# Attention and two expert layers on one core: high parts of the last layer's operands one step ahead of their low parts, and second products in another order

## The chip, the core and the metric

The kernel runs on one core of a Trainium2 chip. Its engines are TensorE (PE, which also loads weights, shown as PEld), VectorE (DVE), ScalarE (ACT), GpSimd (POOL) and SyncE (SP), which here only issues DMAs. Each engine works through its own list of instructions in the order written. The metric is device time of one execution in microseconds (us): the kernel before takes 1069.21 us, the median of 3 runs (1068.4 to 1069.44).

## The reference

```python
def _moe2_ref(x, w_in, w_out, s, b):
    h = x @ w_in                  # 2304 x 512 by 512 x 2048
    r = np.maximum(h, 0.0)
    g = s * (r * r) + b
    return (g @ w_out).astype(np.float32)

def reference(**kwargs):
    attn_out = _attn_ref(**attn_kwargs)          # two softmax attentions
    x = attn_out.transpose(0, 2, 1, 3).reshape(B * S, H * D)
    x = _moe_ref(x=x, **moe_kwargs)              # four experts, weighted sum
    return _moe2_ref(x=x, **moe2_kwargs)         # the last layer
```

Everything is float32. The change lies in the last layer alone, `_moe2_ref`.

## The kernel before

**Stages.** Attention comes first, then the four experts, then the last layer. Every float32 product is made of three reduced-precision matmuls: an operand is split into a high part (ACT copies it, rounded) and a low part (DVE or POOL subtracts the high part from the source), and the products low x high, high x high and high x low are added up in PSUM.

**The last layer.** The 2048 hidden columns are four groups `g` of 512, and the 2304 tokens three passes `tp` of 768. Each pair (group, pass) is a block scheme with seven products in the place of eight, `k` from 0 to 6, named 11, 12, s2, s1, s3, s4 and 22 in the order of work, and each has two column blocks `j`. That makes 4 x 3 x 7 x 2 = 168 steps. One step issues the six matmuls of one first product (`m3`, line 1053, 384 columns each). For a group after the first, nine matmuls of the *second* products of the pass before follow in the same step (`m4_next`, line 1191, 256 columns each). A pass is 14 steps.

**Second products.** They too are seven products in a block scheme, in the order of the tuple `LAST` (line 697). Product `k` takes the gated activation `gg[g, tp, k]` and the weight `wov[g, k]`, and has three row blocks `i` of 128 tokens with six matmuls each: 18 matmuls in two steps. The function `behind` (line 1582) writes this list, row blocks in the order 0, 1, 2. The products form two chains in PSUM. Chain a is 11, s2, s3, 22 and adds up in bank `on_0`; chain b is 12, s1, s4 in bank `on_2`. Row blocks 0 and 2 lie in the chain's bank; row block 1 of both chains lies in one common bank, `on_1`, each chain in its own half. A finished row block is added to the result by DVE (line 1206): once for row block 1 (128x256) and once for row blocks 0 and 2 together (128x512). The next matmul into a bank waits for the write-outs of that bank, whichever half they read.

**What else DVE and ACT do in a pass.** The first products go to SBUF as `z` (DVE lines 1119, ACT lines 1110 to 1128). After step 10 of a pass come its squares (ACT, line 1133) and the scaling by `s` and `b` (ACT, line 1135), then four sums of blocks (DVE, line 1147, tiles `qs` and `z`), then the high part (ACT) and the low part (DVE, line 1159) of each `gg`. These stand in the weave at fixed steps: `q_sum` at steps 16, 16, 18 and 19 counted from the pass's start, `q_part` for product k at step 13 + 2k (high) and 14 + 2k (low), both for k = 0 at 13 and 14 and for k = 1 the same.

**The first-weight operands.** Seven operands `wop[g, k]` per group are made in the last pass of the group before: POOL makes sums of weight blocks (`wi_sums`, lines 774 to 781), and `wop_parts` (line 783) makes high and low parts in two halves `j`, ACT at line 789 (128x256) and DVE at line 790. For operand k both stand at step u0 + 2k + 1, where u0 is the first step of that pass. An operand is used 14 steps after its step u0 + 2k.

**What sets the order.** The order on each engine is the order in which the Python code issues instructions: a dictionary from step to functions (`at`, `run`), then the step's first product, then its nine second products. Nothing reorders it later.

Of the kernel before, what the change touches and what calls it, by code (L numbers as in the profile page):

```python
# [9 lines left out]
F32R = mybir.dt.float32r  # L10
U32 = mybir.dt.uint32
AF = mybir.ActivationFunctionType
ALU = mybir.AluOpType
# [6 lines left out]
def attention_experts_mlp_kernel(  # L20
# [25 lines left out]
    nc = tc.nc  # L46
# [5 lines left out]
    P = 128  # L52
# [12 lines left out]
    NS = T3 // P  # L65
# [5 lines left out]
    keep = ctx.enter_context(tc.tile_pool(name="keep", bufs=1))  # L71
# [10 lines left out]
    def f32(ap):  # L82
        return ap.bitcast(F32)
# [607 lines left out]
    NQ = FG // 2  # L691
    HK = KB // 2

    OPS = ("11", "12", "s2", "s3", "s1", "s4", "22")
    NK = len(OPS)
    ORDER = ("11", "12", "s2", "s1", "s3", "s4", "22")
    LAST = ("12", "11", "s2", "s1", "s3", "s4", "22")
    wi_dram = [dram.tile([P, 2, DM], F32, name=f"wi_dram{q}") for q in range(DFF // P // 2)]
    wo_dram = [dram.tile([P, DM], F32, name=f"wo_dram{fb}") for fb in range(DFF // P)]

# [49 lines left out]
    tw, wop = {}, {}  # L750
# [29 lines left out]
                nc.gpsimd.tensor_tensor(out=t2, in0=t["s4"], in1=t["s1"], op=ALU.subtract)  # L780
                nc.gpsimd.tensor_tensor(out=t4, in0=t4, in1=t2, op=ALU.subtract)

    def wop_parts(g, k):
        n = g * NK + k
        tag = "w1" if n % 8 < 4 else "w1p"
        t = wop[g, k] = keep.tile([P, NQ, 2, HK * P], F32R, tag=tag, bufs=4, name=f"wop{g}{k}")
        for j in range(NQ):
            src = tw[g * NQ + j][(ORDER if g else OPS)[k]]
            nc.scalar.activation(t[:, j, 0], src, AF.Copy)
            nc.vector.tensor_tensor(out=t[:, j, 1], in0=src, in1=f32(t[:, j, 0]), op=ALU.subtract)  # L790

    def wo_tile(fb):
        t = wodd.tile([P, 2, DM], F32R, tag="w1p", bufs=FG, name=f"wo{fb}")
# [33 lines left out]
    def wov_parts(g, k):  # L827
        pool, tag = (gb, "wo") if ((g - 1) * NK + k) % 8 < 4 else (wodd, "w1p")
        t = wov[g, k] = pool.tile([P, 2, 2, HK * P], F32R, tag=tag, bufs=FG, name=f"wov{g}{k}")
        hi, lo, src = t[:, 0], t[:, 1], tv[g][LAST[k]]  # L830
        nc.scalar.activation(hi, src, AF.Copy)
# [318 lines left out]
    def q_part(g, tp, k, n):  # L1150
        src = quad[g, tp][LAST[k]]
        if n == 0:
            gg[g, tp, k] = gb.tile(
                [P, 2, 2, T3], F32R, tag="gg", bufs=6, name=f"gg{g}{tp}{k}"
            )
            nc.scalar.activation(gg[g, tp, k][:, 0], src, AF.Copy)  # L1156
        else:
            t = gg[g, tp, k]
            nc.vector.tensor_tensor(out=t[:, 1], in0=src, in1=f32(t[:, 0]), op=ALU.subtract)  # L1159
# [21 lines left out]
    def m4_next(g, tp, k, i, n):  # L1181
        op = LAST[k]
        b = int(op in ("12", "s1", "s4"))
# [29 lines left out]
    with tc.manual_schedule():  # L1213
# [8 lines left out]
        for gi in range(G):  # L1222
# [3 lines left out]
            out=p_rows[:NB], in_=probs.rearrange("(j a) e -> j (a e)", a=P)  # L1226
# [123 lines left out]
        def at(step, fn, *args):  # L1350
            weave.setdefault(step, []).append((fn, args))
# [76 lines left out]
        for e in range(E):  # L1428
            for bi in range(B):
# [8 lines left out]
                for c in range(4):  # L1438
                    n, gi = divmod(c, 2)
# [43 lines left out]
        for k in (2, 3):  # L1483
            at(s0 + NF + 7 + k, wop_parts, 0, k)
        for what, d in (("s1", 4), ("s2", 5), ("s3", 6)):
            at(s0 + d, x_sum, 0, what)
        def pos(v):

            return len(ua) + v - EARLY
# [7 lines left out]
        for tp in range(NTP):  # L1497
            u0 = tp * UP
# [6 lines left out]
        for g in range(1, NG):  # L1505
            u0 = pos((g * NTP - 1) * UP)
            for q in range(g * NQ, (g + 1) * NQ):
                at(u0 - 5, load_wi, q)
            at(u0 - 2, wi_sums, g, 0)
            for k in range(NK):  # L1510
                at(u0 + 2 * k + 1, wop_parts, g, k)
                if k == 1:
                    at(u0 + 3, wi_sums, g, 1)
                for tp in range(NTP):
                    at(pos((g * NTP + tp) * UP + 2 * k) - 9, xs_load, g, tp, k)
            at(u0 + UP + 1, load_wov, g)
            at(u0 + UP + 4, wov_sums, g, 0)
            at(u0 + UP + 9, wov_sums, g, 1)
            for k in range(NK):
                at(u0 + UP + 6 + 2 * k + 6 * (g == 1 and k > 3), wov_parts, g, k)  # L1520
            for tp in range(NTP):
                i = pos((g * NTP + tp) * UP)
                for j in range(NQ):
                    for d, n in ((3, 0), (9, 3), (11, 1)):
                        at(i + d + j, q_relu, g, tp, j, n)
                    for c in range(2):
                        for n in range(2):
                            at(i + 11 + 2 * c + j + n, q_gate, g, tp, f"{c + 1}{j + 1}", n)
                for n in range(2):
                    for k in range(2):  # L1530
                        at(i + 13 + n, q_part, g, tp, k, n)
                for d, what in ((16, "s1"), (16, "s2"), (18, "s3"), (19, "s4")):
                    at(i + d, q_sum, g, tp, what)
                for k in range(2, NK):
                    for n in range(2):
                        at(i + 13 + 2 * k + n, q_part, g, tp, k, n)
# [45 lines left out]
        def behind(g, tp, *_):  # L1582
            if g == 0:
                return [
                    (m4, g, tp, x, f, n) for x in range(2 * NS) for f in range(FG) for n in range(3)
                ]
            return [
                (m4_next, g, tp, k, x, n)
                for k in range(NK) for x in range(NS) for n in range(6)
            ]  # L1590

        def second(count):
# [57 lines left out]
```

## Time and profile before

| | before |
|---|---|
| median of 3 runs | 1069.21 us (1068.4 to 1069.44) |
| the profiled execution, its time | 1069.46 us |
| its span, first to last instruction | 1067.7 us |
| PE busy | 1046.9 us (98%) |
| DVE, ACT, POOL busy | 687.2, 542.2, 211.2 us |
| second products (line 1191), busy | 157.2 us, 1134 matmuls |
| PE idle before line 1191 | 11.7 us, 11.1 of it ended by DVE line 1206 |

The page of the profile names lines of the kernel as L1191. `on<-wov,gg` is what an instruction writes and reads, by the program's names without buffer numbers. Idle time in square brackets is that of the engine just before the instruction, with what ended it. From 798 us on the second products on PE are those of groups 1 to 3; before that they are those of group 0, which are plain and untouched by the change.

### The profile page before, as it was taken

Reading aid. Unit: us, or ns where it says so; the run is one execution under the profiler, and the core shown is the slowest. Engines: PE = TensorE matmul, PEld = TensorE weight load, DVE = VectorE, ACT = ScalarE, POOL = GpSimd, SP = SyncE. Lnnn points to the kernel's source line nnn. Section 1 sums busy time; section 2 is a strip of 40 time slices with the busy share of each in tenths; the row PEclk is TensorE's granted clock in tenths of the full one; section 3 lists DMA queues with packets and bytes.
Section 4 is the critical chain, followed back from the end, with each engine's and each line's share of the span. In section 5 each row is a group of like instructions: output and inputs, shape, how many; then the busy total and the mean of one; then the engine's idle time right before and its main releaser. Section 6 shows DMA issues by size and latency. Waiting matters only on the chain.

```text
span 1067.7 us, 18211 instructions
## 1 busy us (share of the span) xinstructions
PE 1046.9 (98%) x6701; PEld 924.0 (87%) x6701; DVE 687.2 (64%) x1342; ACT 542.2 (51%) x1165; POOL 211.2 (20%) x222
## 2 busy tenths in 40 slices
PE   8999999999999999999999999999999999999996
PEld 5778888888888888888888888998899899999996
DVE  7885755565664255564365735799536787777776
ACT  3533334533442343443335756766576666766752
POOL 0630330321010321010321122113123142214000
PEclk9999999999999999999999999999999999999999
DMA  9874122986578446584856233347756565565523
GB/s 257 213 127 90 21 91 99 322 223 186 197 250 250 117 121 190 189 250 158 230 141 169 75 104 138 130 193 252 293 178 217 177 207 210 173 210 180 176 89 119
DMA packets 106899, 187.09 MB, mean 175 GB/s; under 512 B 49449, under 2 KB 63785, under 8 KB 106811
## 3 DMA queue, kind: packets, MB, share of 16 engines
q1 hardware_dynamic: 106539, 185.87, 55.9%
q8 instruction: 53, 0.87, 0.3%
q14 instruction: 35, 0.29, 0.1%
q10 hardware_dynamic: 272, 0.07, 0.0%
HBM read 131.11 MB, written 54.79 MB: 174 GB/s over the span
## 4 chain that ended last, share of the span: by engine, by line
PE 80%; ACT 8%; DVE 7%; issue 2%; DMA 2%; SPq 1%; ACTq 0%; DVEq 0%
PE acc L889 35%; PE h L843 19%; PE h L1053 10%; PE on L1191 6%; PE o L1171 5%; ACT z L1133 2%; ACT z L1135 2%; PE pp L625 2%; DVE o_sb L1206 1%; DVE gg L1159 1%; ACT gg L1156 1%; DMA v<-in_v_dram 1%; DVE z L1119 1%; ACT z L1128 1%; DVE wop L790 1%
## 5 line engine op out<-in xcount | busy, mean ns | idle before, releaser
L843 PEld LDWEIGHTS h<-a,w1p 128*128 128x128 f32 x1536 | 229.1, 188 | 26.5 <-issue 5.6
L843 PE MATMUL h<-a,w1p 128*128 128x320 f32 (+1 forms) x1536 | 248.4, 297 | 0.5 <-DVE hl L866 0.4
L866 DVE SCALAR_TENSOR_TENSOR hl<-h,hh 128x256 fp32r<-128x256 f32 x256 | 107.7, 421 | 216.9 <-ACT rest L864 111.0
L864 ACT ACTIVATE hh<-h 128x256 fp32r<-128x256 f32 x256 | 98.8, 386 | 221.5 <-PE h L843 218.6
L1053 PE MATMUL h<-xs,wop 128*128 128x384 f32 x1008 | 203.0, 337 | 0.0
L889 PE MATMUL acc<-w2l,hh 128*128 128x512 f32 x512 | 201.8, 394 | 0.0
L889 PE MATMUL acc<-w2h,hh 128*128 128x512 f32 x512 | 201.3, 393 | 0.0
L889 PE MATMUL acc<-w2h,hl 128*128 128x512 f32 x512 | 200.4, 391 | 0.0
L1053 PEld LDWEIGHTS h<-xs,wop 128*128 128x128 f32 x1008 | 173.0, 188 | 5.0
L1191 PE MATMUL on<-wov,gg 128*128 128x256 f32 x1134 | 157.2, 283 | 11.7 <-DVE o_sb L1206 11.1
L1191 PEld LDWEIGHTS on<-wov,gg 128*128 128x128 f32 x1134 | 148.6, 189 | 17.4 <-DVE o_sb L1206 15.2
L889 PEld LDWEIGHTS acc<-w2h,hl 128*128 128x128 f32 x512 | 96.2, 188 | 22.0
L889 PEld LDWEIGHTS acc<-w2l,hh 128*128 128x128 f32 x512 | 96.4, 188 | 15.0 <-DVE xt L914 0.4
L889 PEld LDWEIGHTS acc<-w2h,hh 128*128 128x128 f32 x512 | 96.3, 188 | 13.2
L1206 DVE TENSOR_TENSOR o_sb<-on,o_sb 128x256 f32<-128x256 f32 x126 | 67.3, 552 | 23.4 <-PE on L1191 22.6
L1171 PE MATMUL o<-wo,gg 128*128 128x512 f32 x216 | 57.2, 395 | 0.0
L688 POOL TENSOR_TENSOR w2l<-w2r,w2h 128x512 fp32r<-128x512 f32 x24 | 31.7, 1329 | 107.2 <-ACT w2h L685 106.4
L1159 DVE TENSOR_TENSOR gg<-z,gg 128x768 fp32r<-128x768 f32 x45 | 47.1, 1064 | 7.9 <-ACT gg L1156 7.9
L1128 ACT ACTIVATE z<-z 128x384 f32<-128x384 f32 x54 | 28.0, 521 | 37.3 <-DVE z L1119 37.1
L1171 PEld LDWEIGHTS o<-wo,gg 128*128 128x128 f32 x216 | 39.9, 188 | 5.9 <-DVE gg L1028 0.2
L633 DVE TENSOR_TENSOR w1o<-pp,w1o 128x512 fp32r<-128x512 f32 x48 | 29.8, 684 | 20.8 <-ACT w1o L632 20.8
L941 ACT ACTIVATE x<-xt 32x384 f32<-32x384 f32 x80 | 41.9, 523 | 1.3
(449 smaller groups left out, 1340.6 us busy)
## 6 DMA issues: line engine op xcount, KB each, us to landing
xs<-xs_dram SPq DMA_DIRECT2D x63, 768.0 KB, 4.2
w1p_dram<-w1o SPq DMA_DIRECT2D x48, 512.0 KB, 4.1
w1p<-w1p_dram SPq DMA_DIRECT2D x192, 128.0 KB, 4.3
xs_dram<-xs SPq DMA_DIRECT2D x21, 768.0 KB, 3.3
w1r<-in_moe_w_dram SPq DMA_DIRECT2D x12, 512.0 KB, 4.4
w2r<-in_moe_w_dram SPq DMA_DIRECT2D x24, 256.0 KB, 5.1
out_dram<-o_sb SPq DMA_DIRECT2D x18, 256.0 KB, 2.3
v<-in_v_dram SPq DMA_DIRECT2D x8, 512.0 KB, 9.1
```

The costliest lines, as they stand in the source:

```text
L688: nc.gpsimd.tensor_tensor(out=lo, in0=raw_t.pop((e, f)), in1=f32(hi), op=ALU.subtract)
L843: nc.tensor.matmul(t[:, : width(bi, hf)], lhsT=w1p_block(e, bi, f, gi, w), rhs=a2[bi][:, x, gi, part(bi, hf)], start=(n == 0), stop=(n == ...
L864: nc.scalar.activation(hi, src, AF.Relu)
L866: nc.vector.scalar_tensor_tensor(out=lo, in0=src, scalar=0.0, in1=f32(hi), op0=ALU.max, op1=ALU.subtract)
L889: nc.tensor.matmul(acc[j], lhsT=x, rhs=w, start=(f == 0 and n == 0), stop=(g == NF - 1 and n == 2),)
L941: nc.scalar.activation(dst[32 * q : 32 * q + 32, a], src[:, q], AF.Copy)
L1053: nc.tensor.matmul(ps, lhsT=w[:, a, col], rhs=x[:, z, m, :], start=(fresh and n == 0), stop=(n == 3 * HK - 1), skip_group_check=chain,)
L1128: nc.scalar.activation(z, z, AF.Relu)
L1159: nc.vector.tensor_tensor(out=t[:, 1], in0=src, in1=f32(t[:, 0]), op=ALU.subtract)
L1171: nc.tensor.matmul(acc, lhsT=lhsT, rhs=w, start=(f == 0 and n == 0), stop=(f == FG - 1 and n == 2),)
L1191: nc.tensor.matmul(ps[:, half], lhsT=gg[g, tp, k][:, x, r, i * P : (i + 1) * P], rhs=wov[g, k][:, w, r, :], start=(n == 0 and i < 2 and (o ...
L1206: nc.vector.tensor_tensor(out=dst, in0=src, in1=dst, op=ALU.add)
```

## The change

Three edits. The tuple `LAST` gets another order: 12, 11, s1, s2, s4, s3, 22. The high parts of `wop[g, k]` for g > 0 are issued at step u0 + 2k instead of u0 + 2k + 1; the low parts stay at u0 + 2k + 1. The row blocks of a second product come in the order 1, 0, 2. `LAST` is also the order in which `q_part` and `wov_parts` make the second products' operands, so these follow it.

```diff
-    LAST = ("12", "11", "s2", "s1", "s3", "s4", "22")
+    LAST = ("12", "11", "s1", "s2", "s4", "s3", "22")
...
-    def wop_parts(g, k):
+    def wop_parts(g, k, which=(0, 1)):
         n = g * NK + k
         tag = "w1" if n % 8 < 4 else "w1p"
-        t = wop[g, k] = keep.tile([P, NQ, 2, HK * P], F32R, tag=tag, bufs=4, name=f"wop{g}{k}")
+        if 0 in which:
+            wop[g, k] = keep.tile([P, NQ, 2, HK * P], F32R, tag=tag, bufs=4, name=f"wop{g}{k}")
+        t = wop[g, k]
         for j in range(NQ):
             src = tw[g * NQ + j][(ORDER if g else OPS)[k]]
-            nc.scalar.activation(t[:, j, 0], src, AF.Copy)
-            nc.vector.tensor_tensor(out=t[:, j, 1], in0=src, in1=f32(t[:, j, 0]), op=ALU.subtract)
+            if 0 in which:
+                nc.scalar.activation(t[:, j, 0], src, AF.Copy)
+            if 1 in which:
+                nc.vector.tensor_tensor(
+                    out=t[:, j, 1], in0=src, in1=f32(t[:, j, 0]), op=ALU.subtract
+                )
...
             for k in range(NK):
-                at(u0 + 2 * k + 1, wop_parts, g, k)
+                for x in range(2):
+                    at(u0 + 2 * k + x, wop_parts, g, k, (x,))
                 if k == 1:
                     at(u0 + 3, wi_sums, g, 1)
...
             return [
                 (m4_next, g, tp, k, x, n)
-                for k in range(NK) for x in range(NS) for n in range(6)
+                for k in range(NK) for x in (1, 0, 2) for n in range(6)
             ]
```

In the changed kernel the lines behind `wop_parts` have numbers higher by 6: 789 is 792, 790 is 794, 1119 is 1125, 1147 is 1153, 1156 is 1162, 1159 is 1165, 1191 is 1197, 1206 is 1212.

Three places of the program show what moves. In the names, wop26 is operand 6 of group 2, gg120 and gg121 are the second products' operands 0 and 1 of group 1, pass 2, z120 the first products' block of that pass with j = 0, and o_sb3 the result of token tile 3. First ACT at the end of group 1's last pass, before:

```order
L1112 ACTIVATE z120_9211<-h1200_9212 128x384
L1133 ACTIVATE z120_9211<-z120_9211 128x768
L1135 ACTIVATE z121_9237<-z121_9237,b_sb_80,s_sb_79 128x768
L1156 ACTIVATE gg120_9522<-z121_9237 128x768
L1156 ACTIVATE gg121_9524<-z120_9211 128x768
L789 ACTIVATE wop26_9528<-wi4_9087 128x256
L789 ACTIVATE wop26_9528<-wi5_9089 128x256
L1112 ACTIVATE z121_9237<-h1201_9238 128x384
```

The same place of ACT in the changed kernel:

```order
L792 ACTIVATE wop26_9504<-wi4_9088 128x256
L792 ACTIVATE wop26_9504<-wi5_9090 128x256
L1118 ACTIVATE z120_9214<-h1200_9215 128x384
L1139 ACTIVATE z120_9214<-z120_9214 128x768
L1141 ACTIVATE z121_9238<-z121_9238,b_sb_80,s_sb_79 128x768
L1162 ACTIVATE gg120_9526<-z121_9238 128x768
L1162 ACTIVATE gg121_9528<-z120_9214 128x768
L1118 ACTIVATE z121_9238<-h1201_9239 128x384
```

The two high parts have moved ahead of five instructions of ACT.

DVE at the start of group 2's second pass, where the sums qs of the pass before stand between the write-outs, before:

```order
L1147 TENSOR_TENSOR qs1_20_9930<-z200_9555,z201_9582 128x768 [waits Activation_49]
L1147 TENSOR_TENSOR qs2_20_9932<-qs1_20_9930,z200_9555 128x768 [waits DVE_49]
L1119 TENSOR_TENSOR z210_9886<-h2110_9934,uv0_7683 128x384 [waits PE_49]
L1119 TENSOR_TENSOR z211_9907<-h2111_9956,uv1_7719 128x384 [waits PE_49,Activation_49]
L1206 TENSOR_TENSOR o_sb5_8891<-on_1_8988,o_sb5_8891 128x256 [waits PE_49]
L1206 TENSOR_TENSOR o_sb5_8891<-on_0_9028,o_sb5_8891 128x2x256 [waits PE_49]
```

And in the changed kernel:

```order
L1153 TENSOR_TENSOR qs1_20_9930<-z200_9555,z201_9583 128x768 [waits Activation_49]
L1153 TENSOR_TENSOR qs2_20_9932<-qs1_20_9930,z200_9555 128x768 [waits DVE_49]
L1125 TENSOR_TENSOR z210_9886<-h2110_9934,uv0_7683 128x384 [waits PE_49]
L1212 TENSOR_TENSOR o_sb5_8891<-on_1_8981,o_sb5_8891 128x256 [waits PE_49]
L1125 TENSOR_TENSOR z211_9908<-h2111_9957,uv1_7719 128x384 [waits PE_49,Activation_49]
L1212 TENSOR_TENSOR o_sb5_8891<-on_0_9035,o_sb5_8891 128x2x256 [waits PE_49]
```

The write-out of row block 1 now stands one add earlier, ahead of z211. The low parts and sums around it keep their places.

PE, one second product (gg121, chain a) with the first products (h) of its two steps, before; on_1 is the common bank of row block 1:

```order
L1053 MATMUL h2030_9696<-xs203_9474,wop23_9381 128x384 [waits DMAHW0_49]
L1053 MATMUL h2030_9696<-xs203_9474,wop23_9381 128x384 x5
L1191 MATMUL on_0_9028<-wov11_8785,gg121_9524 128x256 [waits DVE_49]
L1191 MATMUL on_0_9028<-wov11_8785,gg121_9524 128x256 x5
L1191 MATMUL on_1_8988<-wov11_8785,gg121_9524 128x256 [waits DVE_49]
L1191 MATMUL on_1_8988<-wov11_8785,gg121_9524 128x256 x2
L1053 MATMUL h2031_9718<-xs203_9474,wop23_9381 128x384 x6
L1191 MATMUL on_1_8988<-wov11_8785,gg121_9524 128x256 x3
L1191 MATMUL on_0_9028<-wov11_8785,gg121_9524 128x256 x6
```

And in the changed kernel:

```order
L1059 MATMUL h2030_9696<-xs203_9478,wop23_9359 128x384 [waits DMAHW0_49]
L1059 MATMUL h2030_9696<-xs203_9478,wop23_9359 128x384 x5
L1197 MATMUL on_1_8981<-wov11_8785,gg121_9528 128x256 [waits DVE_49]
L1197 MATMUL on_1_8981<-wov11_8785,gg121_9528 128x256 x5
L1197 MATMUL on_0_9035<-wov11_8785,gg121_9528 128x256 x3
L1059 MATMUL h2031_9719<-xs203_9478,wop23_9359 128x384 x6
L1197 MATMUL on_0_9035<-wov11_8785,gg121_9528 128x256 x9
```

The wait for DVE at row block 1 has moved from the product's seventh matmul to its first, and the write-out that it waits for is issued after the sixth matmul of the product before, not after the twelfth.

## Rows read from the trace of the kernel before

**Rows 1.** The page, busy time and share of the span by engine, with instructions.
```profile
PE 1046.9 (98%) x6701; PEld 924.0 (87%) x6701; DVE 687.2 (64%) x1342; ACT 542.2 (51%) x1165; POOL 211.2 (20%) x222
```

**Rows 2.** Who waited for whom, from 660 us on: total, times, longest (us).
```profile
DVE o_sb L1206 <- PE on L1191: 22.6, 44, 2.0
DVE wop L790 <- ACT wop L789: 22.0, 11, 3.8
...
PEld on L1191 <- DVE o_sb L1206: 15.2, 20, 1.9
...
ACT wop L789 <- POOL wi L780: 1.6, 1, 1.6
```

**Rows 3.** Waits of PEld, from 795:1041, 818:862, 913:957 and 1035:1068 us.
```profile
PEld on L1191 <- DVE o_sb L1206: 12.0, 17, 1.9
...
PEld on L1191 <- DVE o_sb L1206: 4.9, 5, 1.9
...
PEld on L1191 <- DVE o_sb L1206: 4.5, 5, 1.9
...
PEld on L1191 <- DVE o_sb L1206: 3.2, 3, 1.7
```

**Rows 4.** Chain that ended last, 1000 to 1068 us: start, us, what.
```profile
999.94 1.07 PE on L1191 x9
1001.01 1.05 PE h L1053 x6
```

**Rows 5.** Timeline from 847 us: start, us, instruction, idle before.
```profile
851.94 1.58 ACT L1156 ACTIVATE gg<-z 128x768 fp32r<-128x768 f32 x2
...
852.41 0.87 PE L1191 MATMUL on<-wov,gg 128*128 128x256 f32 x6
853.42 0.71 ACT L789 ACTIVATE wop<-wi 128x256 fp32r<-128x256 f32 x2
853.86 0.76 DVE L790 TENSOR_TENSOR wop<-wi,wop 128x256 fp32r<-128x256 f32 x2 [3.78 <-ACT wop L789]
...
854.53 1.02 DVE L1206 TENSOR_TENSOR o_sb<-on,o_sb 128x256 f32<-128x256 f32 x2
...
855.00 0.62 PE L1191 MATMUL on<-wov,gg 128*128 128x256 f32 x3 [1.72 <-DVE o_sb L1206]
```

**Rows 6.** Timeline from 823 us.
```profile
824.05 0.76 DVE L790 TENSOR_TENSOR wop<-wi,wop 128x256 fp32r<-128x256 f32 x2 [2.54 <-ACT wop L789]
...
825.20 0.42 PEld L1191 LDWEIGHTS on<-wov,gg 128*128 128x128 f32 x3 [0.64 <-DVE o_sb L1206]
```

**Rows 7.** Timeline from 884 us.
```profile
890.48 1.28 POOL L832 TENSOR_TENSOR wov<-wv,wov 128x512 fp32r<-128x512 f32 x1 [2.54 <-ACT wov L831]
890.53 2.05 DVE L1147 TENSOR_TENSOR qs<-qs,z 128x768 f32<-128x768 f32 x1
...
892.50 1.01 DVE L1119 TENSOR_TENSOR z<-h,uv 128x384 f32<-128x384 f32 x2
...
893.43 1.01 DVE L1206 TENSOR_TENSOR o_sb<-on,o_sb 128x256 f32<-128x256 f32 x2
...
893.90 0.41 PEld L1191 LDWEIGHTS on<-wov,gg 128*128 128x128 f32 x3 [0.54 <-DVE o_sb L1206]
```

**Rows 8.** Timeline from 1040 us, the end of the kernel.
```profile
1041.72 1.02 DVE L1206 TENSOR_TENSOR o_sb<-on,o_sb 128x256 f32<-128x256 f32 x2
...
1043.68 0.96 DVE L1147 TENSOR_TENSOR qs<-z,z 128x768 f32<-128x768 f32 x1 [0.94 <-ACT z L1135]
...
1045.55 1.01 DVE L1206 TENSOR_TENSOR o_sb<-on,o_sb 128x256 f32<-128x256 f32 x2
...
1046.02 2.38 PE L1191 MATMUL on<-wov,gg 128*128 128x256 f32 x18 [1.44 <-DVE o_sb L1206]
...
1052.12 10.97 PE L1191 MATMUL on<-wov,gg 128*128 128x256 f32 x90 [0.87 <-DVE o_sb L1206]
...
1063.14 0.69 DVE L1206 TENSOR_TENSOR o_sb<-on,o_sb 128x512 f32<-128x512 f32 x1 [0.28 <-PE on L1191]
```

## The prediction

> **What bounds the kernel now.** I read the busy times first, then who waited for whom, then the stretches in which these waits lie, each on a timeline. PE is busy 98% of the span [rows 1], so nothing that another engine does costs time unless PE stands still for it; the whole prize is PE's idle time. From 660 us on nearly all of it has one reason: the weight loads before second products waited 20 times, 15.2 us in all, for the write-outs of line 1206 on DVE [rows 2]. I price a stop by PEld's wait and not by PE's own idle time, because a matmul's modelled end covers part of the stop. Example: six matmuls start at 852.41, nine take 1.07 us when nothing stops them [rows 4], so the next was due at 852.41 + 6 x 0.119 = 853.12. It came at 855.00 [rows 5]: 1.88 us lost, where PE shows 1.72.
>
> Why are the write-outs late? The largest wait of DVE in this part, 22.0 us in 11 pieces, is for ACT at the low parts of `wop` [rows 2]. At 853.86 DVE had stood 3.78 us for a high part that ACT reached at 853.42, behind two `gg` copies of 1.58 us; the write-out came at 854.53, and PE went on at 855.00 [rows 5]. At 824.05 it is the same with 2.54 us of DVE and 0.64 us of PE [rows 6]. So the stops sit where operands of the next group are made: 4.9 us in five stops at group 1 to 2, 4.5 in five at group 2 to 3. Up to 1041 us all stops are 12.0 us in 17 [rows 3], which leaves 2.6 us in seven stops elsewhere. The end, after the last first product, has 3.2 us by PEld in three stops [rows 3], and one more of 0.87 by PE [rows 8].
>
> **The change, part by part.** *High parts one step earlier.* No instruction is added or taken away; per group 14 copies of ACT (0.71 us a pair) move ahead, at wop26 past five instructions. The low part then finds its high part done. At wop26 the five are the two gg copies (1.58 us, so 0.79 for 128x768 elements) and, by the same size as an estimate, 2.0 us for two of 128x768 and one of 128x384. The copy starts near 849.8 instead of 853.42, and DVE, free since 853.86 - 3.78 = 850.08, waits a few tenths; its write-out, which stands ahead of the low part now, does not wait at all. The stop of 1.9 us goes. At 824 the copies pass one instruction of 128x384 and one of 128x768, by the same estimate 1.2 us: DVE loses 2.54 - 1.2 = 1.3 us instead of 2.54, and the stop was 0.64. It goes too. I take the other eight to go with them, since their write-outs are behind the same kind of wait. What is late next there? The sums and gg copies behind are pushed back by at most one pair, 0.71 us, and in the busy stretch another pair has left in front, so their time is about kept. All ten stops gone is 4.9 + 4.5 = 9.4 us.
>
> *A new wait.* The high part of the third operand needs a POOL sum that itself waits for the low parts of the first two. ACT already waited 1.6 us there once, in the change from group 0 to 1 [rows 2]. A step earlier (1.05 + 1.07 = 2.1 us [rows 4], some 3 us in group 0) this is between 0, if the low parts come earlier by as much, and 1.6 + 3 = 4.6 us of ACT. Queued behind it on ACT are copies of first products and gg parts, which the DVE adds wait for, and behind those PE through its banks. In group 0 PE has not one stop on them, so the cover is there. I take 0 and keep 1.5 us per group, 4.5 in all, for the range.
>
> *Row block 1 first, and the new order of products.* These move DVE's write-outs and PE's waits, and cost no instruction. Two adjacent products of chain a (11, s2) had only one first product between them, 1.05 us, for a write-out of 0.69 us and its start; now the adjacent pair (s3, 22) has 1.05 us and six matmuls, 0.71 us. The stops of that kind go. For row block 1 the distance from the write-out's issue to the need grows from 6 + 6 matmuls and one first product (0.71 + 1.05 + 0.71 = 2.5 us) to 3 + 9 and two (0.36 + 1.07 + 2.1 = 3.5 us), as long as DVE is on time.
>
> Where DVE is late for another reason it is the other way round. At 890.53 a sum of DVE takes 2.05 us, while the same form takes 0.96 [rows 7, 8]; a POOL instruction ran from 890.48 to 891.76. Then follow two adds and the write-out at 893.43, and PE lost 0.54 us. In the new order the write-out stands between the two adds, at 892.50 + 0.5 = 893.0, done 893.4; but PE now needs it when the first product is over and not after six matmuls more, at 892.65 (893.90 - 0.54 less 0.71) and not at 893.36. The stop is 0.75 us, more than the 0.54 before. The same sums meet POOL's same work once in group 3. So of the 2.6 us elsewhere I leave two stops of 0.75 and take 1.1 us as gain. The Trainium skill, SBUF — State Buffer, section "SBUF: two separate sides", says that a DVE instruction with two SBUF inputs and a POOL instruction that reads SBUF exclude each other for their whole length. The trace agrees: 891.76 - 890.53 + 0.96 = 2.19 against 2.05. By that rule low parts that no longer wait for ACT can meet POOL's weight sums, and one such meeting costs DVE 1.1 us; the sum takes none.
>
> The stop at row block 1 is one of banks: the wait stands at its first matmul although the other chain's half was written out long before. The Trainium skill, PSUM — Partial Sum Buffer, "PSUM bank collisions raise a hardware error", asks for guarding by bank and quadrant and not by address. If only the half counted, row block 1 could never stop PE and the two stops of 0.75 would be none.
>
> *The end.* Here no wop is made, and DVE waits for ACT's last scaling, 0.94 us until 1043.68 [rows 8]. In the new order the first product of the last pass cannot start until the write-out at 1045.55 (behind two sums) has read bank on_1; PE is there at 1044.4 (1046.02 less 1.44 idle and 0.16 that a modelled end outlasts its step, 1.88 - 1.72) and stops 1.6 us, as before. Product 22 ahead of it, row block 1 first, is due 24 matmuls before 1044.4, at 1041.5, and needs the write-out at 1041.72 done, 0.42 later (1.02 less 0.6 for the pair's second, by estimate): 0.7, which is new. The next two products find their write-outs behind one sum and one gg part (0.96 each) and stop 0.4 to 0.5 each, where the second of them alone stood 0.87. The last product pays 0.3 for the pair s3, 22. That is 0.7 + 1.6 + 0.9 + 0.3 = 3.5, with small ones near 3.9, against 3.2 + 0.87 = 4.1. I take 0.2 of gain, between -1 and 1.5. The last write-out (1063.14) and its transfer to the end of the span stay.
>
> *Restarts.* The three matmuls after a stop take 0.62 us [rows 5]; without it 3 x 0.119 + 0.16 = 0.52. So 0.1 per stop; 15 of the 17 stops vanish, 1.5 us.
>
> *Sum.* 9.4 + 1.1 + 0.2 + 1.5 = 12.2 us. Against the profiled execution, 1069.46 us (its span is 1067.7, the 1.8 around it does not change), that is 1057.3. The median of the runs, 1069.21, lies 0.25 lower; I say 1057.0.
>
> **The rivals.** *Half of it.* The wait moves from the low part of wop to the low part of gg, since ACT is a solid queue there (1.58 us of gg copies directly before the copy at 853.42). Then the stops shrink by what the copy gained and no more: at 824 all, at 853 about half. Some 6 us gained, 1063.5. For it: ACT is the late engine in both stretches. Against: DVE write-outs stand before the gg low parts in the row, not behind. *Better.* The sums miss POOL's instructions in the moved order, and the two stops left go as well; with 1.5 us at the end, 1069.46 - 12.2 - 1.7 - 1.3 = 1054.3. *Nothing.* The copies find their buffer still read by PE (each operand reuses that of the operand eight before), ACT stands there, and DVE with it: 1069. Against: that last reader is a first product of the step before, and ACT runs behind PE here: the copy of 853.42 belongs to the step before the one whose second products run at 852.41. *Slower.* Row block 1 first makes PE ask 0.71 us earlier while the write-out comes only one add, 0.5 us, earlier: 0.2 us lost for each product at which DVE is late. If DVE is late at all 63 products that is 12.6 us, and with the ten stops kept as they are the kernel takes 1082, with them gone 1072.7. It decides from 9.4 / 0.2 = 47 late products on. Against: DVE waited for PE at 44 of 126 write-outs [rows 2], so it is on time at a good part of them.
>
> **How the numbers follow.** Forecast 0.62 (own range 1055.0 to 1060.5); half of it 0.19; better 0.08; nothing 0.06; slower 0.05. The 80% range goes down to 1054.3, the better case, and up to 1063.5, the middle of the half case, since POOL's 4.5 us or a gg wait would lead there. A change under 0.2% (2.1 us) can't be told from none here. Faster: 0.62 + 0.19 + 0.08 = 0.89. Same 0.06, slower 0.05.
>
> **What would show it.** Right: DVE's waits at the wop low part fall from 22.0 us to a few; PEld's waits for the write-outs fall from 15.2 to about 5.5, of which 4 at the end; between 818 and 957 us nothing over 0.3; a stop of about 0.75 at the fifth step of the second pass of groups 2 and 3, at the first matmul of a row block 1. Wrong: long waits of DVE at gg low parts with PE stopping behind them (half of it); ACT waiting for POOL at the third operand by more than 2 us with PE idle; or many small stops at the products' first matmuls (slower).

## The result, and the profile after

The changed kernel takes 1057.91 us (median of 4 runs, 1057.74 to 1058.72), beside 1069.33 for the kernel before on the same chip: a ratio of 0.9896, interval 0.9879 to 0.9913. That is 11.4 us faster by the medians; the forecast was 1057.0. The profiled execution took 1058.72, 10.7 less than the one of before.

The page of the changed kernel, busy time, share of the span and instructions of each engine, answering to [rows 1]:

```profile
PE 1041.7 (99%) x6701; PEld 923.2 (87%) x6701; DVE 685.8 (65%) x1342; ACT 542.3 (51%) x1165; POOL 211.6 (20%) x222
```

The instructions are the same in number, yet PE's busy time fell by 5.2 us and its idle time, span less busy, from 20.8 to 15.2. So only about half of the gain is idle time on this page. Of the 5.2 us of busy time, 3.6 lie behind 700 us (351.4 against 347.8): in the modelled ends of the matmuls ahead of a stop and in the slow matmul behind it. Therefore I measure the stops below by the starts of the matmuls on the timeline: what lies between two neighbouring starts over the 0.119 us (second product) or 0.174 us (first product) of an unstopped matmul. From 700 us on this loss is 18.5 us before and 7.1 after, 11.4 less. The first matmul of the last layer starts at 658.9 us before and at 659.6 here, 0.7 later, although nothing ahead of it was changed. From it to the end of the span it is 408.8 us before and 397.3 here, 11.5 less. These 11.5 less the 0.7 are, within rounding, all of the 10.7 between the two profiled executions.

Who waited for whom in the changed kernel from 660 us on (total, times, longest), answering to [rows 2]:

```profile
DVE o_sb L1212 <- PE on L1197: 36.0, 48, 2.1
...
PE on L1197 <- DVE o_sb L1212: 4.5, 6, 1.4
...
ACT wop L792 <- POOL wi L780: 2.9, 1, 2.9
...
PEld on L1197 <- issue: 2.7, 3, 1.2
...
PEld on L1197 <- ACT gg L1162: 2.1, 2, 1.6
...
DVE wop L794 <- ACT wop L792: 1.5, 2, 0.8
...
PEld on L1197 <- ACT z L1141: 1.0, 1, 1.0
...
PEld on L1197 <- DVE o_sb L1212: 0.3, 1, 0.3
```

DVE's wait for ACT at the low parts fell from 22.0 us to 1.5, and DVE now waits 36.0 us for PE at the write-outs where it was 22.6: it is the early engine. PEld's stops are 2.7 + 2.1 + 1.0 + 0.3 = 6.1 us where they were 15.2. The profile puts them down to other releasers than before, while all six stops that PE itself shows here are ended by the write-out. Hence a total is to be compared over all releasers of a line.

The stretch that answers to [rows 5], one step of the change from group 1 to 2, on the timeline of the changed kernel (start, us, instruction, idle before):

```profile
846.13 0.71 ACT L792 ACTIVATE wop<-wi 128x256 fp32r<-128x256 f32 x2
846.39 0.42 DVE L1212 TENSOR_TENSOR o_sb<-on,o_sb 128x256 f32<-128x256 f32 x1 [0.20 <-PE on L1197]
...
846.73 0.75 DVE L794 TENSOR_TENSOR wop<-wi,wop 128x256 fp32r<-128x256 f32 x2
...
848.87 0.69 DVE L1212 TENSOR_TENSOR o_sb<-on,o_sb 128x512 f32<-128x512 f32 x1 [1.39 <-PE on L1197]
849.05 1.58 ACT L1162 ACTIVATE gg<-z 128x768 fp32r<-128x768 f32 x2
...
849.71 1.23 PE L1197 MATMUL on<-wov,gg 128*128 128x256 f32 x9
849.93 1.83 DVE L1165 TENSOR_TENSOR gg<-z,gg 128x768 fp32r<-128x768 f32 x2 [0.37 <-ACT gg L1162]
```

The copy of wop26 stands 2.92 us before the two gg copies (849.05 - 846.13), where it stood 1.48 behind them. DVE does its low part without a wait. Its write-outs wait for PE and not the other way. PE's nine matmuls take 1.23 us, where the stopped place of [rows 5] had six in 0.87 and three in 0.62 with 1.72 idle between them. Between 818 and 880 us neither PE nor PEld has a wait left before second products.

The two stops that the forecast kept, on the timeline at the second pass of group 2, answering to [rows 7]:

```profile
885.78 1.30 POOL L838 TENSOR_TENSOR wov<-tv,wov 128x512 fp32r<-128x512 f32 x1 [2.52 <-ACT wov L837]
885.83 0.85 ACT L1162 ACTIVATE gg<-qs 128x768 fp32r<-128x768 f32 x1
885.83 2.06 DVE L1153 TENSOR_TENSOR qs<-qs,z 128x768 f32<-128x768 f32 x1
...
887.82 0.54 DVE L1125 TENSOR_TENSOR z<-h,uv 128x384 f32<-128x384 f32 x1
888.29 0.41 DVE L1212 TENSOR_TENSOR o_sb<-on,o_sb 128x256 f32<-128x256 f32 x1
...
888.84 1.30 PE L1197 MATMUL on<-wov,gg 128*128 128x256 f32 x9 [0.90 <-DVE o_sb L1212]
...
889.52 1.30 POOL L838 TENSOR_TENSOR wov<-wv,wov 128x512 fp32r<-128x512 f32 x1 [2.44 <-ACT wov L837]
889.68 1.96 DVE L1153 TENSOR_TENSOR z<-z 128x768 f32<-128x768 f32 x1
```

The chain is as the prediction has it: the second sum `qs` takes 2.06 us beside POOL, an add and the write-out of row block 1 follow, and PE stands at the first matmul behind the first product. By the starts this costs 1.13 us with the slow matmul behind it (1.06 without), and its twin in group 3, at 977.75, 1.03 (0.96); the forecast had 0.75 each.

The end of the changed kernel, answering to [rows 8]:

```profile
1031.78 2.38 PE L1197 MATMUL on<-wov,gg 128*128 128x256 f32 x18 [0.79 <-DVE o_sb L1212]
...
1033.15 0.96 DVE L1153 TENSOR_TENSOR qs<-z,z 128x768 f32<-128x768 f32 x1 [0.92 <-ACT z L1141]
...
1035.58 2.37 PE L1197 MATMUL on<-wov,gg 128*128 128x256 f32 x18 [1.43 <-DVE o_sb L1212]
...
1038.25 2.37 PE L1197 MATMUL on<-wov,gg 128*128 128x256 f32 x18 [0.29 <-DVE o_sb L1212]
...
1040.91 11.47 PE L1197 MATMUL on<-wov,gg 128*128 128x256 f32 x90 [0.29 <-DVE o_sb L1212]
```

By the starts these four stops are 0.95, 1.58, 0.46 and 0.45, and a fifth at 1050.34 is 0.24, all without the slow matmul behind each. The forecast had 0.7, 1.6, twice 0.4 to 0.5, and 0.3.

### The profile page after: what moved, and what is told of

The parts are those of the page before. It is cut to its first block, busy times and chain, and to the rows that moved or that the text cites. A ratio compares the mean times of both kernels' runs of the same rounds, so it can differ in the third digit from the quotient of the medians.

```text
span 1056.9 us, 18211 instructions
## 1 busy us (share of the span) xinstructions
PE 1041.7 (99%) x6701; PEld 923.2 (87%) x6701; DVE 685.8 (65%) x1342; ACT 542.3 (51%) x1165; POOL 211.6 (20%) x222
## 4 chain that ended last, share of the span: by engine, by line
PE 89%; ACT 4%; DVE 2%; DMA 2%; issue 1%; SPq 1%; ACTq 0%
PE acc L895 35%; PE h L849 19%; PE h L1059 15%; PE on L1197 10%; PE o L1177 5%; PE pp L625 2%; ACT z L1141 1%; DMA v<-in_v_dram 1%; PE pw L539 1%; ACT z L1139 1%; PE pv L345 1%; DMA w1p<-w1p_dram 1%; DMA w2r<-in_moe_w_dram 0%; PE s L417 0%; ACT x L947 0%
## 5 line engine op out<-in xcount | busy, mean ns | idle before, releaser
L1197 PE MATMUL on<-wov,gg 128*128 128x256 f32 x1134 | 153.8, 282 | 4.6 <-DVE o_sb L1212 4.5
L633 DVE TENSOR_TENSOR w1o<-pp,w1o 128x512 fp32r<-128x512 f32 x48 | 29.8, 683 | 20.8 <-ACT w1o L632 20.8
```

The source lines that it names most:

```text
L633: nc.vector.tensor_tensor(out=t[:, 1], in0=ps[x, z], in1=f32(t[:, 0]), op=ALU.subtract)
L1197: nc.tensor.matmul(ps[:, half], lhsT=gg[g, tp, k][:, x, r, i * P : (i + 1) * P], rhs=wov[g, k][:, w, r, :], start=(n == 0 and i < 2 and (o ...
```

## The experiments

The edits are shown against the changed kernel. The kernels of the row blocks alone, of the order alone and of both reorderings were written from the kernel before, so their lines have its numbers. Where an expectation names theories by letters, A is the prediction's own and the others are its rivals. *Loss* means PE's loss from 700 us on by the starts, as above: 18.5 us before, 7.1 after. The *ten stops* are those of the prediction, in the stretches 818 to 862 and 913 to 957 us of the kernel before, where operands of the next group are made.

**The early high parts alone.** Product order and row blocks as before.

```diff
-    LAST = ("12", "11", "s1", "s2", "s4", "s3", "22")
+    LAST = ("12", "11", "s2", "s1", "s3", "s4", "22")
...
-                for k in range(NK) for x in (1, 0, 2) for n in range(6)
+                for k in range(NK) for x in range(NS) for n in range(6)
```

> The kernel before with only the high parts of wop one step earlier; order of products and row blocks as before. Theory A (the prediction's sum: DVE's wait for ACT at the low parts is the cause of the ten stops between 818 and 957 us): DVE's wait for wop falls from 22.0 us to under 4, the ten stops (9.4 us) go, the seven others (2.6 us) and the end (4.1 us) stay: 1059 to 1060.5 us. Theory B (row block 1 first takes the stops away, by putting the write-out ahead of the low part; the high parts only matter beside it): most of the ten stops stay, 1064 to 1068 us. Theory C (each of the two edits takes most of the same stops): as A.

Measured: 1061.09 beside 1069.63, ratio 0.9916 (0.9903 to 0.993), which is 9.0 us. The prediction's term for this edit is 9.4, and 1.0 of restarts for ten stops beside it. The waits from 660 us on:

```profile
PEld on L1197 <- DVE o_sb L1212: 6.5, 12, 1.6
...
PE on L1197 <- DVE o_sb L1212: 4.3, 7, 1.4
...
DVE wop L794 <- ACT wop L792: 3.1, 4, 1.2
```

The wait at `wop` falls from 22.0 us to 3.1 with this edit alone, and the ten stops go but for three small ones of 0.3 to 0.5 by PEld's waits. The loss is 9.4 us, 4.7 of it from 1000 us on, as before. This run alone does not tell whether the other edits are worth little by themselves.

**Row block 1 first, alone.** High and low parts in one step, product order of before.

```diff
-                for x in range(2):
-                    at(u0 + 2 * k + x, wop_parts, g, k, (x,))
+                at(u0 + 2 * k + 1, wop_parts, g, k)
...
-    LAST = ("12", "11", "s1", "s2", "s4", "s3", "22")
+    LAST = ("12", "11", "s2", "s1", "s3", "s4", "22")
```

> The kernel before with only the row blocks in the order 1, 0, 2. Theory A: DVE still waits some 20 us for ACT at the low parts, the ten stops stay or shrink little, of the seven others 1.1 us go: 1066 to 1069 us. Theory B: about as the whole change, 1058 to 1060 us. Theory C: the write-out of row block 1 stands ahead of the waiting low part, so the stops before it go, but the write-out of row blocks 0 and 2 and the next products come late behind it: the 1.9 us stops become about 1.0, the others under 0.4, 6 to 8 us gained, 1061 to 1063.5 us.

Measured: 1063.27 beside 1069.63, ratio 0.9938 (0.9925 to 0.995), 6.4 us by the medians, although nothing is done about the wait at `wop`. The waits from 660 us on:

```profile
DVE wop L790 <- ACT wop L789: 19.3, 11, 3.8
...
PE on L1191 <- DVE o_sb L1206: 8.7, 12, 1.4
```

And its timeline where [rows 5] has the stop of 1.88:

```profile
852.10 0.76 DVE L790 TENSOR_TENSOR wop<-wi,wop 128x256 fp32r<-128x256 f32 x2 [3.77 <-ACT wop L789]
...
852.77 0.68 DVE L1206 TENSOR_TENSOR o_sb<-on,o_sb 128x512 f32<-128x512 f32 x1
...
853.38 1.82 DVE L1159 TENSOR_TENSOR gg<-z,gg 128x768 fp32r<-128x768 f32 x2
...
855.11 1.01 DVE L1206 TENSOR_TENSOR o_sb<-on,o_sb 128x256 f32<-128x256 f32 x2
...
855.67 1.30 PE L1191 MATMUL on<-wov,gg 128*128 128x256 f32 x9 [1.04 <-DVE o_sb L1206]
```

DVE stands 3.77 us as before (3.78), but the write-out behind it at 852.77 stops nobody: PE needs it later. What stops PE is the next one, at 855.11, behind two gg low parts: 1.2 us by the starts. In the stretches of the ten stops six with 5.2 us are left. So the longer distance between write-out and need takes away part of the same stops that the early high parts take away: each edit alone cures a good part of them, and what the second adds is smaller than what it is worth alone.

**The order of the products alone, and both reorderings without the early high parts.** Both have high and low parts in one step again:

```diff
-                for x in range(2):
-                    at(u0 + 2 * k + x, wop_parts, g, k, (x,))
+                at(u0 + 2 * k + 1, wop_parts, g, k)
```

and the first, which keeps of the change only the line `LAST`, has this too:

```diff
-                for k in range(NK) for x in (1, 0, 2) for n in range(6)
+                for k in range(NK) for x in range(NS) for n in range(6)
```

> The kernel before with only the tuple LAST changed (12, 11, s1, s2, s4, s3, 22). All theories: the ten stops stay. The pair 11, s2 of one chain is gone but the pair s3, 22 has the same distance of one first product with the old row blocks, so the small stops of 0.3 us only move: 1068 to 1070 us. If the order of products mattered by itself (sums ready in another order), the end would be shorter by 1 us or more: below 1068.

> The changed kernel without the earlier high parts (row blocks 1, 0, 2 and the new LAST). Theory A: 9 us slower than the changed kernel, 1066 to 1068 us. Theory B: as the changed kernel, 1058 us. Theory C: as the row blocks alone, 1061 to 1063.5 us, and the difference to the changed kernel (3 to 5 us) is what the earlier high parts are worth once the row blocks are turned.

Measured: the order alone 1070.01, ratio 0.9998 (0.9989 to 1.0006), nothing by the medians. Both reorderings 1063.84, ratio 0.9945 (0.9932 to 0.9957), as the row blocks alone, with a loss of 12.5 us in both. The waits from 660 us on, of the order alone and of both:

```profile
DVE wop L790 <- ACT wop L789: 21.4, 11, 3.8
...
PE on L1191 <- DVE o_sb L1206: 11.1, 9, 1.8
```

```profile
DVE wop L790 <- ACT wop L789: 18.8, 11, 3.8
...
PE on L1191 <- DVE o_sb L1206: 8.7, 10, 1.6
```

The order alone is not nothing in its trace. Its profiled execution, 1067.56 us at a mean granted clock of 1.000, is the fastest of its eleven, and its last layer is 2.0 us shorter than that of before. The other ten, 1068.42 to 1071.09 us, had a mean granted clock of 0.996 to 0.998, where twelve of the fifteen of the kernel before had 0.999 or 1.000. No trace of those ten was kept, so it is not shown where they lost time. The table compares the profiled executions without what lies ahead of the last layer, which differs between executions. It gives time saved against the kernel before (us), from the layer's first matmul to the end of the span, and in parts that begin and end at the same matmul in each kernel:

| kernel | last layer | stretches of the ten stops | the other second products, to 1035 us of before | the end |
|---|---|---|---|---|
| early high parts alone | 9.1 | 9.0 | 0.0 | 0.0 |
| row blocks alone | 6.0 | 4.0 | 1.4 | 0.6 |
| order alone | 2.0 | 0.7 | 1.4 | 0.0 |
| row blocks and order | 6.1 | 4.5 | 1.4 | 0.2 |
| all three | 11.5 | 9.8 | 1.4 | 0.2 |

The three edits alone add up to 17.1 us, together they give 11.5. In the stretches of the ten stops the early high parts and the row blocks both cure the same stops. At the other second products each of the two reorderings alone gives all of the 1.4.

**The changed kernel once more**, with no edit, to stand beside the three kernels below that move POOL's weight parts, the two sums, or the low parts.

> The changed kernel once more, beside the three others of this batch. All theories: 1057 to 1059 us, 0.989 to 0.990 of the kernel before.

Measured: 1058.43 beside 1069.29, ratio 0.9895 (0.988 to 0.991), loss 7.0 us.

**POOL's weight parts moved away from the `qs` sums.** The last two `wov_parts` of groups 2 and 3 (a high part on ACT, line 837, and a low part on POOL, line 838) come four steps later.

```diff
-                at(u0 + UP + 6 + 2 * k + 6 * (g == 1 and k > 3), wov_parts, g, k)
+                at(u0 + UP + 6 + 2 * k + 6 * (g == 1 and k > 3) + 4 * (g > 1 and k > 4), wov_parts, g, k)
```

> The changed kernel with POOL's and ACT's parts of the second-product weights 5 and 6 of groups 2 and 3 four steps later. Theory (the two stops of about 1 us that are left outside the end come from a DVE sum held for 1.1 us by a POOL instruction): the second sum of the first pass of groups 2 and 3 takes 0.96 us and not 2.06, both stops go, 2.1 to 2.3 us less than the changed kernel, 1055 to 1056.5 us. Rival (they come from row block 1 first, which asks 0.71 us earlier; DVE is late there anyway behind ACT's scaling): the sum may be short, but stops of 0.5 us or more stay, under 1 us gained.

Measured: 1056.69, ratio 0.9875 (0.986 to 0.9891), 1.7 us below the changed kernel beside it. Its timeline at the place of the stop of 1.13:

```profile
885.49 0.96 DVE L1153 TENSOR_TENSOR qs<-qs,z 128x768 f32<-128x768 f32 x1
...
886.36 0.55 DVE L1125 TENSOR_TENSOR z<-h,uv 128x384 f32<-128x384 f32 x1
...
886.83 0.41 DVE L1212 TENSOR_TENSOR o_sb<-on,o_sb 128x256 f32<-128x256 f32 x1
...
887.45 1.25 PE L1197 MATMUL on<-wov,gg 128*128 128x256 f32 x9
```

The same sum takes 0.96 us with no POOL instruction beside it, and PE does not stop. Both stops are gone (loss 4.9, nearly all of it at the end). The sum starts at the same place as in the changed kernel, 226.2 us after the layer's first matmul in both, and ends 1.1 earlier. So these two stops are the price of that meeting, and the step of the prediction on them is shown.

**The two sums one step later instead.** POOL is left where it was.

```diff
-                for d, what in ((16, "s1"), (16, "s2"), (18, "s3"), (19, "s4")):
+                for d, what in ((17, "s1"), (17, "s2"), (18, "s3"), (19, "s4")):
```

> The changed kernel with the sums s1 and s2 of a pass at step 17 in the place of 16, that is behind the write-out of row block 1 of product 22. Theory (DVE late by the held sum): the held sum stands behind that write-out, so the stop of 1.0 us at the next product goes, but the sums, a gg part and then the next write-out are as late as before and the product after stops 0.5 to 0.6: about 1 us gained in all, 1056 to 1057.5 us. At the end the stop of 1.6 us at the first product of the last pass goes and comes back at the next one. Rival (row block 1 first alone is the reason): both stops go, 2 us gained, and 1.5 us more at the end, 1054 to 1055.5 us.

Measured: 1055.83, ratio 0.9869 (0.9852 to 0.9885), loss 4.6, 2.6 us below the changed kernel beside it. The timeline at the same place:

```profile
884.37 0.42 DVE L1212 TENSOR_TENSOR o_sb<-on,o_sb 128x256 f32<-128x256 f32 x1
...
885.69 1.30 POOL L838 TENSOR_TENSOR wov<-tv,wov 128x512 fp32r<-128x512 f32 x1 [2.53 <-ACT wov L837]
...
885.74 2.06 DVE L1153 TENSOR_TENSOR qs<-qs,z 128x768 f32<-128x768 f32 x1
...
887.68 1.23 PE L1197 MATMUL on<-wov,gg 128*128 128x256 f32 x9
...
888.19 0.68 DVE L1212 TENSOR_TENSOR o_sb<-on,o_sb 128x512 f32<-128x512 f32 x1
...
889.79 1.23 PE L1197 MATMUL on<-wov,gg 128*128 128x256 f32 x9
```

The sum still takes 2.06 us beside POOL, but the write-out of row block 1 now stands ahead of it in DVE's list, and PE does not stop. I had expected a smaller stop at the next product, behind the sum, and about 1 us gained in all. There is no such stop: the write-out of 888.19 is done at 888.87, and PE's next nine start at 889.79. At the end the stop of 1.58 went and came back as 1.74 at the product behind it, as expected.

**Both of these.**

```diff
-                at(u0 + UP + 6 + 2 * k + 6 * (g == 1 and k > 3), wov_parts, g, k)
+                at(u0 + UP + 6 + 2 * k + 6 * (g == 1 and k > 3) + 4 * (g > 1 and k > 4), wov_parts, g, k)
...
-                for d, what in ((16, "s1"), (16, "s2"), (18, "s3"), (19, "s4")):
+                for d, what in ((17, "s1"), (17, "s2"), (18, "s3"), (19, "s4")):
```

> The changed kernel with both the later POOL parts and the sums s1, s2 at step 17. Theory (both edits remove the same two stops): as each alone, 1055 to 1056.5 us. Rival (they have separate gains): 1054 us or less.

Measured: 1056.90, ratio 0.9871 (0.9845 to 0.9896), loss 4.7: no better than either. Its last layer takes 394.8 us, with the sums moved alone 394.8, with POOL moved alone 395.1. They cure the same two stops.

**High parts in their old step, low parts one step later.** The distance between the two is that of the change, and nothing comes earlier; POOL's second sums move one step with them.

```diff
-                    at(u0 + 2 * k + x, wop_parts, g, k, (x,))
+                    at(u0 + 2 * k + 1 + x, wop_parts, g, k, (x,))
                 if k == 1:
-                    at(u0 + 3, wi_sums, g, 1)
+                    at(u0 + 4, wi_sums, g, 1)
```

> The changed kernel with the high parts at their old step u0 + 2k + 1 and the low parts a step later, u0 + 2k + 2 (POOL's second weight sum a step later with them). Theory A (what counts is that the low part is issued a step behind its high part, so that DVE does not stand for ACT): the ten stops stay away, DVE waits under 3 us for wop, 1057 to 1059.5 us. Rival (what counts is that ACT makes the high parts early, out of its busy stretch before the gg copies): DVE's waits at gg copies or sums come later by 0.7 us, stops of 0.5 to 1 us come back in both stretches, 1060 to 1062 us.

Measured: 1059.20, ratio 0.9904 (0.9889 to 0.9919), loss 8.1. The waits from 660 us on:

```profile
ACT wop L792 <- POOL wi L780: 8.7, 3, 3.2
...
PE on L1197 <- DVE o_sb L1212: 5.4, 6, 1.4
...
DVE wop L794 <- ACT wop L792: 0.2, 1, 0.2
```

The ten stops stay away: the two stretches take as long as in the changed kernel to 0.01 us. So the cure is the step between the parts, not that ACT does its copy early. ACT's wait for POOL, which the prediction priced as a risk, stood here three times with 8.7 us, and PE has no stop behind any of them. What is dearer than in the change are the two stops beside POOL, 1.52 and 1.45 where the change has 1.06 and 0.96: the first of the two sums starts behind a scaling of ACT that DVE awaited 1.8 us, 1.4 in the change.

**The end.** The two sums at 17, the third at 21, and the low parts of the first two gg at 15 and 16.

```diff
-                        at(i + 13 + n, q_part, g, tp, k, n)
-                for d, what in ((16, "s1"), (16, "s2"), (18, "s3"), (19, "s4")):
+                        at(i + 13 + (2 + k if n else 0), q_part, g, tp, k, n)
+                for d, what in ((17, "s1"), (17, "s2"), (21, "s3"), (19, "s4")):
```

> The changed kernel with DVE's list around the start of a pass sorted by when PE needs each item: sums s1, s2 at step 17 (as before in this study), sum s3 at 21 in the place of 18, low parts of gg 0 and 1 at steps 15 and 16 in the place of 14. Theory (what is left is the order of DVE's work before each write-out of row block 1): the stops of 0.95, 1.58 and 0.45 us at the end become under 0.4, near 0 and about 0.8, none outside the end: 1053.5 to 1055 us. Rival (the end is bound by DVE's total work there, 20 us against 19.6 of PE): the stops only move to later products, 1055.5 to 1056.5 us, as with the sums alone.

Measured: 1055.38 beside 1069.79, ratio 0.9865 (0.9845 to 0.9886), the fastest median of all, though not to be told from the sums at 17. Its profiled execution has a loss of 4.3 us. The end on its timeline:

```profile
1033.41 2.35 PE L1197 MATMUL on<-wov,gg 128*128 128x256 f32 x18 [1.50 <-DVE o_sb L1212]
...
1036.07 2.39 PE L1197 MATMUL on<-wov,gg 128*128 128x256 f32 x18 [0.32 <-DVE o_sb L1212]
...
1038.74 9.32 PE L1197 MATMUL on<-wov,gg 128*128 128x256 f32 x72 [0.28 <-DVE o_sb L1212]
```

The stop of 0.95 became 0.24, as the expectation's theory has it. The one of 1.58, which should have gone nearly to 0, is there with 1.66 at another product, as its rival has it. The loss from 1000 us on is 3.6 to 4.3 us in every version here with row block 1 first (4.2 in the changed kernel, 3.6 in this one) and 4.5 to 4.8 in those without. That the end is bound by the sum of DVE's work between its wait for ACT and the last write-out, and that reordering only moves the stops, fits this. No run that leaves out work of DVE there was made, so it is not shown.

## Why the prediction was right

*The ten stops* (9.4 us). Right in mechanism, and near in size: the early high parts alone gave 9.0 by ratio and by the last layer, the wait at `wop` fell to 3.1 us there and to 1.5 in the change, and in the change no stop is left where the ten stood. With ten restarts the prediction had 10.4; the two stretches gave 9.8 in the change. By the starts the ten stops are 8.8 us, so PEld's waits price them 0.6 too high. The place in the list that the prediction reads (the copy behind two gg copies) moved as it says, 2.92 us ahead. The late-low experiment adds what the prediction did not say: for these stops a step between the parts is all that counts.

*The new wait* (0 taken). Right. It came, 2.9 us, and 8.7 in the late-low kernel, and PE did not stop for it.

*The rows and the order of products* (1.1 us). Right as what they add to the early high parts: 1061.09 against 1057.91 and 1058.43, by ratios 2.0 to 2.1 thousandths or some 2.2 us, by the last layer 2.3, where this term, the end (0.2) and the restarts of five stops (0.5) make 1.8. At the other second products the term and its restarts are 1.6 against 1.4 measured. But the size of the term holds only for one order of counting. Taken first, the row blocks are worth 6.6 us by ratio and the early high parts behind both reorderings only some 5.3 (0.9945 against 0.9895). The prediction's sum gave all of the shared stops to the first edit without saying that the second would have had part of them. A reader who had asked what row block 1 first is worth by itself would have taken 1.1 from it and been wrong by 5.5. Nor does the prediction say that at the other second products one of the two reorderings is enough. Its step on the distance, 2.5 to 3.5 us, was the hint: a stop behind a late write-out shrinks by up to 1.0 whatever made it late.

*The two stops left* (0.75 each). Right in place and cause, which moving POOL away shows; mis-sized at 1.13 and 1.03, 0.66 us in all. From the slow sum's start to the end of the write-out it is 2.87 us as reckoned (893.4 - 890.53 there, 888.70 - 885.83 here). Three small things were left out: PE asked 0.17 sooner (887.78, six starts of 0.174 behind 886.73, so 1.95 us after the sum's start and not 2.12), it started 0.14 after the write-out's end, and the matmuls behind the stop lost 0.07. These make the 0.38 between 0.75 and 1.13. The mark that nothing over 0.3 be left from 818 to 957 us was ill drawn, since the kept stop of group 2 falls into it; between 818 and 880, and from 900 to 970, it holds. By the rule of mutual exclusion in the Trainium skill, SBUF — State Buffer, section "SBUF: two separate sides", the sum would end 0.96 after POOL's end, an estimate of 885.78 + 1.30 + 0.96 - 885.83 = 2.21 us against 2.06 measured; the third sum at 889.68 would take 2.10 and took 1.96. The trace agrees to 0.15 us, and with POOL away the sum takes 0.96. That the stop is one of banks and not of halves agrees with where PE stands: the product there is 12, whose row block 1 goes to chain b's half, and the write-out it waits for is that of product 22, which reads chain a's half. No run here gave the two halves banks of their own, so it is not shown that the stops would then go.

*The end* (0.2 gain). Right. All five stops came, with 3.7 us against 3.5 of the text. With restarts the loss is 4.2 from 1000 us on, against the 4.7 that before has there by the same measure; counted from the matmul at 1035 us of before, 0.2 are gained, as forecast. The order of the products alone gained nothing there, the row blocks alone 0.6.

*Restarts* (1.5 us). No experiment separates them from the stops, but the starts do: the matmuls behind a stop lose 0.07 to 0.13 us together. That is 2.4 us for the 24 stops of over 0.13 us before and 0.5 for the 7 after: 1.9 less, where the prediction had 1.5 for 15 stops.

*The sum.* Set against the last layer's 11.5 us, the forecast's 12.2 is the ten stops with restarts (10.4, measured 9.8), the other second products with restarts (1.6, measured 1.4) and the end (0.2, measured 0.2). No term is off by more than 0.6, so the number does not rest on errors that cancel.

*The rivals.* Half of it fell: DVE waits 0.37 us at the gg low part at 849.93 and PE does not stop behind it. Nothing fell: ACT's copies wait for POOL once, 2.9 us, and for a first product of PE once, 0.7, while DVE's own wait at them is 1.5 us in all. Slower fell most clearly, in the row blocks alone: PE asks 0.71 earlier there too, and the kernel is 6.6 us faster. Better is what the experiments then made: with the two stops gone 1056.69, 1055.83 and 1055.38, where the forecast of that case, with 1.5 us more at the end, was 1054.3.

## What to carry to other kernels

When one engine makes the first half of a pair and another the second, look at what stands ahead of the first in its engine's list: a step between the two halves took the second engine's wait away here, and with it that of the engine that needed its next instruction. A step later for the second half did as well for these stops as a step earlier for the first. Two edits that relax the same late instruction, one at the source and one by a later need, need not add up, so price each alone and both together. Of a stop behind a late write-out look first at what stands between the delay and the write-out on its engine: moving the slow sum behind the write-out was worth as much as making the sum fast.

## What the runs showed that was not expected

PE's page hides about half of what its stops cost: 11.4 us went by the starts of its matmuls, 5.6 by its idle time, 6.9 if the first 100 us are left out. And what lies ahead of the last layer, which no kernel here touches, varied: the layer's first matmul starts at 658.1 us in the profiled execution of the end's kernel and at 661.9 in that of both of these, where the granted clock in the first 100 us is 0.97 and in the others 1.00. That is 3.7 us between executions, as much as the smaller edits are worth. The last layer itself takes the same to 0.02 us in the two profiled executions of the changed kernel. So the smaller edits are read from medians and from stretches, never from two spans, and a median can hide them too, as that of the order alone does.
